# Attention with a threshold and four experts on one core: fewer and larger q/k transfers, R by heads, fillers in other banks, a held pace, highs on GpSimd

## The chip, the cores and the metric

The kernel runs on one core of a Trainium2 chip. The time is the device time in microseconds of one execution. A run of several executions gives a median; the profile is of one execution, recorded apart.

## The reference

```python
scores = scale * q @ k.T                        # 4 batches, 8 heads, 576 x 64, scale = 1/8
thresh = max(scores, axis=-1) - tau
scores = where(scores >= thresh, scores, -1e9)
attn = softmax(scores)                          # + 1e-9 under the fraction
x = (attn @ v).transpose(0, 2, 1, 3).reshape(2304, 512)
p = domain_probs / (domain_probs.sum(-1) + 1e-9)
for e in range(4):                              # w1[e]: 512 x 1024, w2[e]: 1024 x 512
    out += p[:, e] * (relu(x @ w1[e]) @ w2[e])
```

All inputs and the output are fp32.

## The kernel before

The matmuls of experts 0 and 1 are made from halves: a number is scaled by a power of two (from a sum of squares, so that fp16 can hold it), its **high** is the fp16 rounding, its **low** the rest, and a product is high x high + high x low + low x high. The power is found by `squares` (one instruction with an accumulator for each block), `total` (a matmul with ones that adds over partitions) and `pow2` (five small DVE steps).

Attention runs in 80 **items**, each 128 rows of q of a pair of heads (or the 64 tail rows of it): scores into the one score tile `S` (PE, lines 1004 to 1016), scaling and row minimum into `SS` (DVE, line 1066), the threshold by GpSimd (line 1079), the exponent by ScalarE (line 1087), the mask and the row sum by DVE (line 1096). Batch 0 goes in fp32 with turns on PE into the `b` banks (`t_prep`) and the `ma` banks. In later batches q and k are loaded (`t_load`), squared (`t_bound`), split into R16 (`t_turn`: highs on ScalarE, lows on DVE, line 771) and turned by a transposing DMA into T; the probabilities are split and turned the same way (`spread`, lines 1216, 1222 and 1179) into `PT`, and `av` (lines 1335 to 1349) takes them and v.

As soon as a 128- or 256-row part of x is whole, `unit` runs experts 0 and 1 over it (lines 1454 and 1496). When attention has ended, `w_pair` prepares the weights of experts 2 and 3 in pairs of blocks; their sums of squares go through PE into the bank `QA`. From then on `unit7` runs experts 2 and 3 by seven products in place of eight (lines 1690 and 1770).

The order of the work on each engine is made by `Plan` before anything is emitted. Every operation is recorded with an engine, an assumed duration, what it reads and writes, the buffers it uses and a priority. `Plan.schedule` then plays them through: whichever operation is ready, has its buffers and has the lowest priority number is placed next. Numbers such as `LATE` (added to a transposing DMA), `SLACK` (added to a wait between engines after the time `SLACK0`) and `pl.hold` (item i doesn't start before 6.0 us x i) only shift what stands where in the order; no wait is written into the program by them. The same holds for the assumed durations and for `port`, by which the planner lets DVE and GpSimd hold each other up. When PE has nothing ready and was busy less than `KEEP` of the recent past, the planner puts in a **filler**: four 112-column matmuls of the identity (line 1843) into columns 848 to 959 of the score tile.

Expert weights come in blocks of 128 hidden units, 128 x 1024 numbers. `w_prep` (experts 0 and 1) takes the squares, the power, the highs (line 911, ScalarE) and the lows (line 936, DVE). `on_gp` names blocks whose lows GpSimd makes instead, in two instructions: scale in place (line 919) and subtract (line 928). For expert 1 these are the four even blocks, by `GP1`.

SP's queue issues nearly all transfers, in one order: loads, stores and the transposing DMAs of R and of the probabilities.

Of the kernel before, what the change touches and what calls it, by code (L numbers as in the profile page):

```python
# [22 lines left out]
class Plan:  # L23
# [18 lines left out]
    SLACK, SLACK0, LATE, seed = {}, 0, 0, 0  # L42
# [87 lines left out]
    def schedule(self):  # L130
# [44 lines left out]
        while True:  # L175
            progress = True
            while progress:
                progress = False
                for e in engines:
# [13 lines left out]
                    if pick is None:  # L193
                        if e == "PE" and self.fill and self.fill[0] <= now < self.fill[1] and (
# [107 lines left out]
def topk_attention_moe_kernel(  # L302
# [61 lines left out]
    kind("raw", "raw", "raw", [128, 8, 2, D], FP32)  # L364
# [73 lines left out]
    def chain_tile(key, prio):
        nonlocal n_am
        if prio >= 5:  # L440
            return ("AM", key)
# [6 lines left out]
    for name in ("TP", "ET0"):  # L448
# [90 lines left out]
    def pow2(src, s_out, p_out, r, w, use, prio, tmp, au, add=None):  # L539
# [3 lines left out]
        def step(fn, rr, ww, more=()):  # L543
            dve(150, fn, rr, ww, use=use + list(more), prio=prio)
# [103 lines left out]
    def t_load(g, prio, kd="raw"):  # L648
        b, pr = divmod(g, NP)
        u = [(kd, ("qk", g))]  # L650
        for i, src in enumerate((q, k)):
# [10 lines left out]
            for h in range(2):  # L662
                load(
                    lambda i=i, h=h: pl.t(*u[0])[:, 4 * i:4 * i + 4, h, :],
                    lambda src=src, h=h: src[b, 2 * pr + h, 0:SM, :].rearrange(
                        "(p j) d -> p j d", j=4
                    ),
                    131072, [("rawqk", g, i, h)], use=u, prio=prio, issue=650, rate=175.0,
                )

    def t_bound(g, prio):
# [147 lines left out]
    def v_prep(b, loaded, prio):  # L819
        st, V = ("st", ("v", b)), ("vr", b)  # L820
        vu, view, parts = loaded
        for i in range(NP):
# [223 lines left out]
    def item(i):  # L1046
# [957 lines left out]
```

## Time and profile before

| | |
|---|---|
| median of 3 runs | 982.22 us (981.32 to 983.5) |
| profiled execution | 983.57 us, span 981.7 us |
| PE busy | 953.0 us (97% of the span) |
| DVE busy | 733.6 us (75%) |
| ACT busy | 556.5 us (57%) |
| GpSimd (POOL) busy | 257.5 us (26%) |
| fillers on PE | 228 matmuls |

The span runs from the first to the last instruction on the core. Matmuls follow each other in a pipeline, and the end of each is modelled, so a busy PE can still lose time between two of them. The granted clock is the share of TensorE's full clock that was given in a stretch. A row's "idle before" is time in which that engine stood still just ahead of the instructions of the row, and what ended it.

### The profile page before, as it was taken

What the parts mean: (1) busy time and instruction counts of PE and PEld (TensorE: products, weight loads), DVE (VectorE), ACT (ScalarE), POOL (GpSimd) and SP (SyncE); (2) the same over time, 40 slices, a digit from 0 to 9 for tenths busy, and PEclk for the clock granted to TensorE, in tenths of its full rate; (3) what the DMA queues carried; (4) which work ended last, traced back from release to release, by engine and by line L of the source; (5) the groups of instructions that cost most, each with busy time, mean ns of one, the idle gap of its engine ahead of it and who ended that gap; (6) DMA issues with size and microseconds to landing.
All of it is one profiled execution on the core that took longest, in us unless ns stands there. A gap on an engine that the chain in (4) does not pass through costs nothing.

```text
span 981.7 us, 20793 instructions
## 1 busy us (share of the span) xinstructions
PE 953.0 (97%) x7796; PEld 625.1 (64%) x7796; DVE 733.6 (75%) x1826; ACT 556.5 (57%) x1181; POOL 257.5 (26%) x400
## 2 busy tenths in 40 slices
PE   8799999999998999999999999999999999999998
PEld 6576655566655656566566756776666667666663
DVE  4799979999888988999763725897665588655551
ACT  5897877777777778786656758532222233212120
POOL 1155643354343344343332422200000010000000
PEclk9999999999999999999999999999999999999999
DMA  7812437778899679966662223301100102001001
GB/s 232 253 56 55 93 79 181 142 123 149 162 179 171 97 149 160 201 119 141 99 112 94 93 82 106 108 12 45 54 33 23 65 23 76 12 1 55 33 1 43
DMA packets 237397, 96.04 MB, mean 98 GB/s; under 512 B 201712, under 2 KB 224240, under 8 KB 237296
## 3 DMA queue, kind: packets, MB, share of 16 engines
q1 hardware_dynamic: 236208, 94.05, 43.1%
q8 instruction: 61, 1.00, 0.4%
q10 hardware_dynamic: 1088, 0.66, 0.2%
q14 instruction: 40, 0.33, 0.1%
HBM read 40.41 MB, written 14.16 MB: 56 GB/s over the span
## 4 chain that ended last, share of the span: by engine, by line
PE 77%; DVE 8%; DMA 7%; ACT 4%; issue 2%; SPq 1%; POOL 0%; DVEq 0%; ACTq 0%; POOLq 0%
PE mm L1770 19%; PE Q L1690 17%; PE mm L1496 16%; PE mm L1454 13%; PE S L1004 5%; PE av L1335 4%; DMA wraw<-in_moe_w_dram 3%; DVE E L1096 1%; DMA T<-R 1%; PE av L1344 1%; PE S L1010 1%; DVE SS L1066 1%; SPq L504 1%; DMA PT<-E 1%; ACT E L1087 1%
## 5 line engine op out<-in xcount | busy, mean ns | idle before, releaser
L1770 PE MATMUL mm<-WP,h 128*128 128x512 f16 x864 | 221.7, 379 | 0.0
L1496 PE MATMUL mm<-W,h 128*128 128x512 f16 x864 | 208.0, 381 | 0.1
L1454 PEld LDWEIGHTS <-W 128*128 128x128 f16 x2016 | 174.5, 98 | 31.4 <-issue 1.8
L1690 PEld LDWEIGHTS <-WP 128*128 128x128 f16 x1680 | 153.5, 98 | 63.5 <-issue 0.2
L1731 ACT ACTIVATE h<-qt 128x256 f16<-128x256 f32 (+1 forms) x160 | 62.1, 394 | 216.0 <-DVE qt L1710 215.6
L1454 PE MATMUL mm<-X,W 128*128 128x256 f16 (+1 forms) x1632 | 181.3, 267 | 0.0
L1710 DVE SCALAR_TENSOR_TENSOR qt<-Q,wc,qt 128x256 f32<-128x256 f32 (+1 forms) x280 | 124.2, 453 | 60.8 <-PE Q L1690 57.9
L1481 POOL TENSOR_TENSOR h<-hr,h 128x256 f16<-128x256 f32 (+1 forms) x168 | 130.1, 780 | 134.0 <-ACT h L1474 105.1
L1096 DVE SCALAR_TENSOR_TENSOR E<-SS,sm,E 128x576 f32<-128x576 f32 x144 | 123.7, 869 | 12.8 <-ACT E L1087 6.6
L1496 PEld LDWEIGHTS <-h 128*128 128x128 f16 x864 | 81.8, 99 | 77.9 <-issue 3.4
L1079 POOL TENSOR_SCALAR sm<-sm,tau_p 128x1 f32<-128x1 f32 x144 | 76.5, 532 | 184.1 <-DVE SS L1066 119.4
L1087 ACT ACTIVATE E<-SS,sm 128x576 f32<-128x576 f32 x144 | 109.1, 769 | 26.0 <-DVE SS L1066 17.6
L1770 PEld LDWEIGHTS <-h 128*128 128x128 f16 x864 | 82.9, 98 | 54.9
L1690 PE MATMUL Q<-T,WP 128*128 128x256 f16 (+1 forms) x960 | 117.8, 262 | 0.0
L1216 ACT ACTIVATE E<-E,ri 128x576 f16<-128x576 f32 (+1 forms) x120 | 83.1, 723 | 28.7 <-DVE ri L1194 11.4
L1222 DVE SCALAR_TENSOR_TENSOR E<-E,ri,E 128x576 f16<-128x576 f32 (+1 forms) x120 | 89.8, 779 | 8.6 <-ACT E L1216 8.0
L1066 DVE TENSOR_SCALAR_CACHE_REDUCE SS<-S,qc 128x576 f32<-128x576 f32 x108 | 85.7, 808 | 8.6 <-PE S L1010 3.4
L1466 ACT ACTIVATE hr<-mm,wc 128x256 f32<-128x256 f32 (+1 forms) x168 | 72.6, 435 | 33.4 <-PE mm L1454 30.5
L1690 PE MATMUL Q<-X,WP 128*128 128x256 f16 (+1 forms) x720 | 88.9, 262 | 0.0
L1647 POOL TENSOR_SCALAR psc<-pnv,wpm 128x2 f32<-128x2 f32 (+1 forms) x20 | 10.1, 505 | 287.2 <-DVE acc L1788 260.4
L1738 DVE SCALAR_TENSOR_TENSOR h<-qt,h 128x256 f16<-128x256 f32 (+1 forms) x160 | 61.4, 393 | 28.1 <-ACT h L1731 26.1
L1004 PE MATMUL S<-T 64*128 64x512 f16 (+3 forms) x440 | 71.8, 427 | 4.3 <-DVE SS L1066 4.0
(146 smaller groups left out, 1021.6 us busy)
## 6 DMA issues: line engine op xcount, KB each, us to landing
wraw<-in_moe_w_dram SPq DMA_DIRECT2D x64, 256.0 KB, 4.3
part<-acc SPq DMA_DIRECT2D x18, 256.0 KB, 2.6
X<-x_dram SPq DMA_DIRECT2D x9, 512.0 KB, 3.7
acc<-part SPq DMA_DIRECT2D x18, 256.0 KB, 3.9
out_dram<-acc SPq DMA_DIRECT2D x16, 256.0 KB, 2.3
x_dram<-X SPq DMA_DIRECT2D x7, 512.0 KB, 3.1
vr<-in_v_dram SPq DMA_DIRECT2D x12, 256.0 KB, 5.4
raw<-in_q_dram SPq DMA_DIRECT2D x24, 128.0 KB, 3.1
```

The lines of the kernel that those rows point to most:

```text
L1004: nc.tensor.matmul(ps[:, 1024 * h:1024 * h + SM] if j < 4 else ps[rows(h), 0:SM], qm(h, a), km(h, c), start=(y == 0), stop=(y == last),)
L1066: nc.vector.tensor_scalar(out=pl.t(*ssu)[:, S * h:S * h + S], in0=pl.t(*su)[:, 960 * h:960 * h + S], scalar1=qc[:, g, 2:3] if g >= NP * T3 ...
L1087: lambda h=h: nc.scalar.activation(out=pl.t(*eu)[:, S * h:S * h + S], in_=pl.t(*ssu)[:, S * h:S * h + S], func=ACTF.Exp, scale=-1.0, bias= ...
L1096: lambda h=h, col=col: nc.vector.scalar_tensor_tensor(out=pl.t(*eu)[:, S * h:S * h + S], in0=pl.t(*ssu)[:, S * h:S * h + S], scalar=pl.t(* ...
L1216: nc.scalar.activation(out=o, in_=e, func=ACTF.Copy, scale=pl.t(*ru)[:, h:h + 1])
L1222: nc.vector.scalar_tensor_tensor(out=o, in0=e, scalar=pl.t(*ru)[:, h:h + 1], in1=hh, op0=ALU.mult, op1=ALU.subtract,)
L1454: nc.tensor.matmul(ps[:, 0:n], w[:, wp, 0, c * 128:(c + 1) * 128], x[:, c, xp, c0:c0 + n], start=(i == 0), stop=(i == len(seq) - 1),)
L1481: lambda hu=hu, hru=hru: nc.gpsimd.tensor_tensor(out=pl.t(*hu)[:, 1, 0:n], in0=pl.t(*hru)[:, 0:n], in1=pl.t(*hu)[:, 0, 0:n], op=ALU.subtra ...
L1496: nc.tensor.matmul(ps, h[:, hp, 128 * i:128 * i + 128], w[:, wp, 1, :], start=(f == f0 and hp == 0 and wp == 0), stop=(f == f1 - 1 and hp ...
L1690: nc.tensor.matmul(reg(r), w[:, wp, o:o + 128], xb(b, c, xp), start=(n == 0), stop=(n == 5),)
L1710: lambda: nc.vector.scalar_tensor_tensor(out=tmp(o), in0=reg(r), scalar=wcs, in1=tmp(i), op0=ALU.mult, op1=ALU.add),
L1770: nc.tensor.matmul(ps, ht()[:, hp, 128 * i:128 * i + 128], w[:, wp, o:o + 512], start=(f == 0 and hp == 0 and wp == 0), stop=(f == NF - 1 ...
```

## The change

- `t_load`: q and k of a pair of heads in batches 1 to 3 each come in one transfer of 256 KB (pieces of 1 KB) instead of two of 128 KB (pieces of 256 bytes). The raw tile now has the two heads apart.
- `t_turn`: highs and lows of R head by head, 512 columns each, instead of 1024 at once. `t_bound` squares the same numbers.
- Fillers, and the sums of the early `total`s, go into a `b` bank that is free at the time (`ID`, `AMB`) instead of the score tile. Fillers end for good when the first expert matmul is placed.
- `w_prep`: the highs of expert 0's eight blocks are made by GpSimd; `GP1` names no block any more, so DVE makes all 16 lows.
- `v_prep`: all 16 squares of v on ScalarE instead of DVE.
- The planner's numbers: hold 6.7 us x i - 40 us, `LATE` 1500 (was 1200), `LATL` 1500 for loads (new), `SLACK` 100 for DVE and ACT from 10 us on, a seed that varies each assumed duration by about 3%, other assumed durations for a few DVE steps, `port` for the small scales of `unit`.

`P32 = 12` names the same 12 groups, those of batch 0, that `V32` named.

```diff
@@ schedule
-                        if e == "PE" and self.fill and self.fill[0] <= now < self.fill[1] and (
+                        if e == "PE" and self.fill and filling and spare["b"] and self.fill[0] <= now < self.fill[1] and (
...
+                        filling = filling and self.kinds[u[0]][0] != "mm"
...
+                        elif now >= self.SLACK0:
+                            end += self.LATL
...
-    pl.LATE = 1200
-    pl.SLACK0 = 60000
-    pl.seed = 0
+    pl.LATE, pl.LATL = 1500, 1500
+    pl.SLACK0 = 10000
+    pl.seed = 5
...
-    kind("raw", "raw", "raw", [128, 8, 2, D], FP32)
+    kind("raw", "raw", "raw", [128, 2, 8, D], FP32)
@@ t_load
-            for h in range(2):
-                load(
-                    lambda i=i, h=h: pl.t(*u[0])[:, 4 * i:4 * i + 4, h, :],
-                    lambda src=src, h=h: src[b, 2 * pr + h, 0:SM, :].rearrange(
-                        "(p j) d -> p j d", j=4
-                    ),
-                    131072, [("rawqk", g, i, h)], use=u, prio=prio, issue=650, rate=175.0,
-                )
+            load(
+                lambda i=i: pl.t(*u[0])[:, :, 4 * i:4 * i + 4].rearrange("p h j d -> p h (j d)"),
+                lambda src=src: src[b, 2 * pr:2 * pr + 2, 0:SM, :].rearrange(
+                    "h (p j) d -> p h (j d)", j=4
+                ),
+                262144, [("rawqk", g, i)], use=u, prio=prio,
+            )
@@ t_turn
-        for c, n, u in ((0, 1024, ru), (8, 256, tl)):
+        for c, n, u in ((0, 512, ru), (4, 512, ru), (8, 256, tl)):
@@ v_prep
-                lambda: junk[:, 0:9 * D], parts, [("vm", b, i)], [vu[i], st], prio, i in (0, 1, 2, 3),
+                lambda: junk[:, 0:9 * D], parts, [("vm", b, i)], [vu[i], st], prio, i in (),
@@ w_prep
-            act(
+            if (e, f) in tuple((0,f) for f in range(8)):
+                gp(
+                    1116,
+                    lambda u=u, W=W, f=f: nc.gpsimd.tensor_scalar(
+                        out=pl.t(*W)[:, 0], in0=pl.t(*u), scalar1=wsc[:, e, f:f + 1],
+                        scalar2=1.0, op0=ALU.mult, op1=ALU.mult,
+                    ),
+                    rr, [("wh", e, f)], use=[u, W], prio=prio(f),
+                )
+            else:
+              act(
@@ item
-        pl.hold[o] = (0,6.0)[0] + 1000 * (0,6.0)[1] * i
+        pl.hold[o] = (-40000,6.7)[0] + 1000 * (-40000,6.7)[1] * i
@@ the main part
-        def idle():
+        def idle(t):
             for _ in range(4):
-                nc.tensor.matmul(s_all[:, 848:960], ident16, ident16[:, 0:112], start=True, stop=True)
+                nc.tensor.matmul(t[:, 0:112], ident16, ident16[:, 0:112], start=True, stop=True)
...
-        GP1 = lambda f: f % 2 == 0
+        GP1 = lambda f: f in ()
```

Three places in the order. On GpSimd (POOL) in the early stage, before: thresholds `sm`, the differences `h` of the first unit, and between them the pair of expert 1's first blocks (lines 919 and 928).

```order
L1079 TENSOR_SCALAR sm<-sm,tau_p 128x1
L1481 TENSOR_TENSOR h<-hr,h 128x128
L919 TENSOR_SCALAR wraw_789<-wraw_789,wsc 128x1024
L1481 TENSOR_TENSOR h<-hr,h 128x128
L928 TENSOR_TENSOR W<-wraw_789,W 128x1024
L1481 TENSOR_TENSOR h<-hr,h 128x128
```

And of the changed kernel, on the same engine, a little earlier (`W<-wraw` are the highs of expert 0's blocks):

```order
L1095 TENSOR_SCALAR sm<-sm,tau_p 128x1 x6
L917 TENSOR_SCALAR W<-wraw_369,wsc 128x1024
L917 TENSOR_SCALAR W<-wraw_382,wsc 128x1024
L917 TENSOR_SCALAR W<-wraw_400,wsc 128x1024
L917 TENSOR_SCALAR W<-wraw_416,wsc 128x1024
L1095 TENSOR_SCALAR sm<-sm,tau_p 128x1 x2
L917 TENSOR_SCALAR W<-wraw_426,wsc 128x1024
L917 TENSOR_SCALAR W<-wraw_459,wsc 128x1024
```

Four highs stand in a row ahead of two thresholds, two more behind them; the pairs of expert 1 are gone.

On DVE, the first lows of expert 0, before (`x` is the scaled `av`, `X` its low):

```order
L936 SCALAR_TENSOR_TENSOR W<-wraw_359,wsc,W 128x1024
L1390 TENSOR_TENSOR X<-x_634,X 128x128
L936 SCALAR_TENSOR_TENSOR W<-wraw_363,wsc,W 128x1024
L936 SCALAR_TENSOR_TENSOR W<-wraw_385,wsc,W 128x1024
L936 SCALAR_TENSOR_TENSOR W<-wraw_403,wsc,W 128x1024
```

And now:

```order
L951 SCALAR_TENSOR_TENSOR W<-wraw_369,wsc,W 128x1024
L1406 TENSOR_TENSOR X<-x_696,X 128x128
L951 SCALAR_TENSOR_TENSOR W<-wraw_382,wsc,W 128x1024
L951 SCALAR_TENSOR_TENSOR W<-wraw_400,wsc,W 128x1024
L1382 SCALAR_TENSOR_TENSOR x_785<-av,v_c,rb 128x128
L951 SCALAR_TENSOR_TENSOR W<-wraw_416,wsc,W 128x1024
```

The lows stand as before, nearly back to back; each reads a high that now comes from GpSimd.

On SP's queue, loads of batch 1's q and k among the first transposes of R, before:

```order
L504 DMA raw<-in_q_dram 128x4x64 x2
L504 DMA raw<-in_k_dram 128x4x64 x2
L780 DMA_TRANSPOSE T_1806<-R_1787 128x10x128
L504 DMA raw<-in_q_dram 128x4x64
L780 DMA_TRANSPOSE T_1806<-R_1787 128x10x128
L504 DMA raw<-in_q_dram 128x4x64
L504 DMA raw<-in_k_dram 128x4x64 x2
```

And now:

```order
L505 DMA raw<-in_q_dram 128x2x256
L505 DMA raw<-in_k_dram 128x2x256
L783 DMA_TRANSPOSE T_1917<-R_1864 128x10x128
L505 DMA raw<-in_q_dram 128x2x256
L783 DMA_TRANSPOSE T_1917<-R_1864 128x10x128
L505 DMA raw<-in_k_dram 128x2x256
```

The transposes stand where they stood, with half as many loads between them.

## Rows read from the trace of the kernel before

**Rows 1.** Windows: stretch, length, busy (instructions) per engine, granted clock, DMA share, GB/s.
```profile
50.00:110.00 60.00, 56.91 (x616) 40.36 (x614) 58.15 (x154) 51.13 (x112) 37.36 (x47) 1.00 0.21 55
110.00:520.00 410.00, 401.00 (x3434) 251.49 (x3433) 355.12 (x919) 306.85 (x641) 168.79 (x262) 1.00 0.75 141
520.00:625.00 105.00, 101.99 (x791) 69.39 (x790) 58.08 (x121) 74.18 (x154) 33.79 (x48) 0.98 0.27 89
625.00:975.00 350.00, 350.00 (x2526) 232.77 (x2524) 229.76 (x533) 90.81 (x214) 9.49 (x18) 1.00 0.12 38
```

**Rows 2.** Windows of the fillers alone (line 1843): PE, PEld, granted clock, DMA.
```profile
60.00:80.00 20.00, 0.00 (x0) 0.00 (x0) 1.00 0.17 54
80.00:100.00 20.00, 2.88 (x52) 2.81 (x52) 1.00 0.26 67
```

**Rows 3.** Waits of PE: for whom, us in total, times, longest.
```profile
PE av L1335 <- DMA PT<-E: 4.1, 4, 1.7
PE S L1004 <- DVE SS L1066: 4.0, 4, 1.6
...
PE QA L533 <- ACT WP L523: 2.2, 1, 2.2
```

**Rows 4.** Windows around the granted clock.
```profile
80.00:90.00 10.00, 7.87 (x82) 5.44 (x79) 8.93 (x13) 6.44 (x13) 7.79 (x5) 1.00 0.40 106
300.00:315.00 15.00, 11.47 (x95) 7.44 (x94) 10.93 (x26) 10.15 (x26) 6.45 (x9) 0.89 0.85 158
565.00:575.00 10.00, 7.75 (x39) 3.98 (x37) 4.42 (x15) 4.80 (x10) 2.42 (x4) 0.83 0.23 75
```

**Rows 5.** Groups by line, batch 0's score reads: count, busy, mean, idle before.
```profile
L1066 DVE TENSOR_SCALAR_CACHE_REDUCE SS<-S,qs 128x576 f32<-128x576 f32 x36 | 28.7, 808 | 5.0 <-PE S L1010 3.3 <-PE S L1843 1.6
```

**Rows 6.** Line 514, squares on DVE: ns min/median/max, first and last start, forms.
```profile
L514 DVE SCALAR_TENSOR_TENSOR junk<-vr x12: 745/750/1158, 94.7 to 331.6; 128x576 f16<-128x576 f32 x12
L514 DVE DVE_READ_ACCUMULATOR junk<-vr x12: 75/80/85, 95.4 to 332.2; 128x1 f32 x12
```

**Rows 7.** Timeline of DVE beside GpSimd's pairs: start, us, instruction.
```profile
70.38 3.15 DVE L936 SCALAR_TENSOR_TENSOR W<-wraw,wsc,W 128x1024 f16<-128x1024 f32 x1
...
80.79 1.98 DVE L562 TENSOR_SCALAR wsc<-st 128x2 int32<-128x2 int32 x1
...
86.80 2.38 DVE L936 SCALAR_TENSOR_TENSOR W<-wraw,wsc,W 128x1024 f16<-128x1024 f32 x1 [0.28 <-ACT W L911]
...
105.13 2.68 DVE L1096 SCALAR_TENSOR_TENSOR E<-SS,sm,E 128x576 f32<-128x576 f32 x1
```

**Rows 8.** Timeline of DVE, the same instructions earlier, undisturbed.
```profile
35.24 0.17 DVE L562 TENSOR_SCALAR wsc<-st 128x4 int32<-128x4 int32 x1
35.39 0.81 DVE L1096 SCALAR_TENSOR_TENSOR E<-SS,sm,E 128x576 f32<-128x576 f32 x1
...
37.87 1.27 DVE L936 SCALAR_TENSOR_TENSOR W<-wraw,wsc,W 128x1024 f16<-128x1024 f32 x1
```

**Rows 9.** Line 919, GpSimd's scale of a block: ns min/median/max.
```profile
L919 POOL TENSOR_SCALAR wraw<-wraw,wsc x4: 1116/1288/1772, 68.5 to 100.8; 128x1024 f32<-128x1024 f32 x4
```

**Rows 10.** DMA issues: count, KB each, median us from issue to landing.
```profile
raw<-in_q_dram SPq DMA_DIRECT2D x24, 128.0 KB, 3.1
...
raw<-in_q_dram SPq DMA_DIRECT2D x4, 256.0 KB, 3.8
```

**Rows 11.** Line 771, lows of R: ns min/median/max.
```profile
L771 DVE SCALAR_TENSOR_TENSOR R<-raw,qc,R x12: 1279/1283/1286, 112.7 to 402.4; 128x1024 f16<-128x1024 f32 x12
L771 DVE SCALAR_TENSOR_TENSOR R<-tl,qc,R x12: 473/484/893, 113.9 to 403.6; 128x256 f16<-128x256 f32 x12
```

**Rows 12.** Timeline of PE behind the last `av`.
```profile
524.87 10.52 PE L1496 MATMUL mm<-W,h 128*128 128x512 f16 x48
535.23 4.09 PE L1454 MATMUL mm<-X,W 128*128 128x256 f16 x36
...
569.88 0.38 PE L533 MATMUL QA<-st,ones 128*128 128x2 f32 x2 [2.25 <-ACT WP L523]
```

More of the change, by code (lines that the diff above doesn't have):

```diff
@@ L41 @@
     FREED, LANES, EARLY = 55, 8, 8000
-    SLACK, SLACK0, LATE, seed = {}, 0, 0, 0
+    SLACK, SLACK0, LATE, LATL, seed = {}, 0, 0, 0, 0
     START, DONE, HELD, FIRST = 600, 800, {714: 1450}, 2200
@@ L328, in topk_attention_moe_kernel @@
     pl = Plan()
-    pl.SLACK = {"PE": 700, "DVE": 0, "ACT": 0,
+    pl.SLACK = {"PE": 700, "DVE": 100, "ACT": 100,
                 "s": 0, "b": 0, "ma": 0, "mm": 0, "q": 0}
-    pl.LATE = 1200
-    pl.SLACK0 = 60000
-    pl.seed = 0
+    pl.LATE, pl.LATL = 1500, 1500
+    pl.SLACK0 = 10000
+    pl.seed = 5
     first = ctx.enter_context(ExitStack())
@@ L447, in topk_attention_moe_kernel @@
     pools["b"] = early
-    for name in ("TP", "ET0"):
+    for name in ("TP", "ET0", "ID", "AMB"):
         kind(name, "b", "b", [128, 512], FP32)
@@ L543, in step @@
         def step(fn, rr, ww, more=()):
-            dve(150, fn, rr, ww, use=use + list(more), prio=prio)
+            o = dve(205, fn, rr, ww, use=use + list(more), prio=prio)
+            if more and more[0][0] == "AMB":
+                b_users.append(o)
         if add:
@@ L674, in t_bound @@
         keys = (
-            [("rawqk", g, i, h) for i in range(2) for h in range(2)]
+            [("rawqk", g, i) for i in range(2)]
             + [("tl", b, i, 0) for i in range(3)] + [("tz", b)]
@@ L751, in t_turn @@
         keys = (
-            [("rawqk", g, i, h) for i in range(2) for h in range(2)]
+            [("rawqk", g, i) for i in range(2)]
             + [("tl", b, i, 0) for i in range(3)] + [("tz", b)]
@@ L850, in v_prep @@
         gp(600, go, ["pn", ("vp", b)], [("pnv", b)], prio=prio)
-        for pr in range(NP) if b >= V32 else ():
+        if b < V32 and P32 == 12:
+            return
+        prio += 8 if b < V32 else 0
+        for pr in range(NP):
             u = ("V", (b, pr))
@@ L1052, in item @@
             ("T16" if g >= NP * T32 else "T", g), ("S", i), ("SS", i), ("E", i), ("sm", i),
-            ("rt", gi) if g // NP < V32 else ("ri", i),
-            ("PT32" if g // NP < V32 else "PT", gi),
+            ("rt", gi) if gi < P32 else ("ri", i),
+            ("PT32" if gi < P32 else "PT", gi),
         )
-        one = g // NP < V32
+        one = gi < P32
         heads = range(2) if j < 4 else range(1)
@@ L1261, in group @@
         ru, bu, au, xu, pu, V = (
-            ("rt", gi), ("rb", gi), ("av", gi), ("x32", gi), ("PT32" if b < V32 else "PT", gi),
-            ("V32" if b < V32 else "V", (b, pr)),
+            ("rt", gi), ("rb", gi), ("av", gi), ("x32", gi), ("PT32" if gi < P32 else "PT", gi),
+            ("V32" if gi < P32 else "V", (b, pr)),
         )
         r16 = ("r16", gi)
-        one = b < V32
+        one = gi < P32
         def rec():
@@ L1328, in av_ @@
             vv, av, t = pl.t(*V), pl.t(*au), pl.t(*pu)
-            pairs = ((0, 0),) if b < V32 else ((0, 0), (0, 1), (1, 0))
+            pairs = ((0, 0),) if one else ((0, 0), (0, 1), (1, 0))
             ts = lambda r, tp, c, c0, c1: t[r, c, tp, c0:c1] if one else t[r, tp, c, c0:c1]
-            va = (lambda r, vp, x: vv[r, x, :]) if b < V32 else (lambda r, vp, x: vv[r, vp, x, :])
+            va = (lambda r, vp, x: vv[r, x, :]) if one else (lambda r, vp, x: vv[r, vp, x, :])
             for c in range(4):
@@ L1342, in av_ @@
                     r = slice(64 * h, 64 * h + 64)
-                    k = n if b < V32 or not h else nm
+                    k = n if one or not h else nm
                     nc.tensor.matmul(
```

58 lines of the change are left out of this document (29 added, 29 removed).

## The prediction

> **What bounds the kernel now.** I read the busy times by stage first, then what TensorE (PE) waited for, then the rows of the places that the diff touches. By stage [rows 1], PE is busy 56.9 of 60 us from 50 to 110, 401.0 of 410 from 110 to 520, 102.0 of 105 from 520 to 625 and 350.0 of 350 from 625 to 975. From 625 on there is nothing to win but order. Before that, the reader is to see two regimes. From 50 to 110 VectorE (DVE) is busy 58.15 of 60, so DVE sets the pace, and part of PE's busy time is fillers: 2.88 us of them from 80 to 100 alone [rows 2]. From 110 on PE is the bound, DVE has 355.1 of 410 and ScalarE (ACT) 306.9 of 410 [rows 1], and what PE loses it loses in single waits: 4.1 us for transposed probabilities (`av`), 4.0 us for the score bank that DVE has not read (`S`), 2.2 us for a sum of squares of expert 2's weights (`QA`) [rows 3]. After the longest ones the granted clock is down: 0.89 over 300 to 315, 0.83 over 565 to 575 [rows 4], which is (1 - 0.89) x 15 = 1.7 us and (1 - 0.83) x 10 = 1.7 us of matmul time.
>
> **The early stage (up to 110 us), where DVE counts.** Five edits meet there.
> 1. Fillers and chain sums leave the score tile for the `b` banks. DVE waited 1.6 us for fillers before it could read scores [rows 5]. That wait goes: -1.6. The fillers fall from 228 to 172 by the order, and none stands behind the first expert matmul, where 92 did.
> 2. The squares of v go to ACT: eight of batches 0 and 1 fall in this stage, each 0.75 us and 0.08 us for its accumulator [rows 6]: 8 x 0.83 = -6.6 on DVE.
> 3. GpSimd's pair for four blocks of expert 1 (scale, then subtract) goes. Beside it DVE instructions took far longer than alone: 3.15 and 2.38 against 1.27 for a low of W, 1.98 against 0.17 for a step of a power, 2.68 against 0.81 for an exponent's mask [rows 7, 8]. Together 1.9 + 1.1 + 1.8 + 1.9 = 6.7 us that come back: -6.7.
> 4. The four lows go to DVE instead: 4 x 1.27 [rows 8] = +5.1.
> 5. The eight highs of expert 0 move from ACT to GpSimd. The trace has no such instruction; nearest is GpSimd's scale of the same 128x1024 block, 1.12 to 1.77 us [rows 9]. In the order four of them stand in a row, and DVE's four lows, which stood back to back, each follow a high, so from the second high on each pair is likely to take turns instead of overlapping: 6 x 1.12 = +6.7. Lower bound 0 (a low starts between two highs, GpSimd waits), upper bound 8 x 1.77 = +14.2. I take 6.7: [rows 7] show four such waits of 1.1 to 1.9 us each, so a whole short one is the nearest. ACT gives up eight highs of 1024 columns and takes eight squares of 576; it has 8.9 us free in the 60 [rows 1], so I cost that at nothing.
>
> The Trainium skill ("SBUF — State Buffer", section "Who interferes with whom") speaks against edit 5: a DVE instruction with two SBUF inputs and a GpSimd instruction that reads SBUF block each other whole, whoever is second. [Rows 7, 8] agree: a low of 1.27 us became 3.15 beside GpSimd's subtraction. By the rule alone all eight highs would wait in turn with the lows, which is the upper end above rather than my 6.7.
>
> Sum on DVE: -1.6 - 6.6 - 6.7 + 5.1 + 6.7 = -3.1. Before 50 us the stage is bound by loads as well, so I pass on half: **-1.5**. Bounds: -9.8 (no lock) to +4.4 (the full lock).
>
> **The middle (110 to 520).** q and k come in one transfer per pair: 24 issues instead of 48 on SP's queue, pieces of 1 KB instead of 256 bytes. 128 KB in small pieces took 3.1 us to land, 256 KB in large ones 3.8 [rows 10], so a pair's q is whole after 3.8 us rather than after two transfers in a row. What waits behind these issues on SP are the transposes of R and of the probabilities, and they are what `av` and, through T, `S` wait for. The two waits are 8.1 us [rows 3], and the dip at 300 another 1.7. The trace doesn't say how much of this the loads cause: between 0 and -9.8. The planner now also counts loads and transposes later (`LATE` and `LATL` 1500, `SLACK` 100), which places the consumer further behind. I take half: **-4.9**. The Trainium skill ("DMA: Bandwidth & Descriptors", "Specifications") puts the smallest piece at line rate at 512 bytes; by it the old loads paid extra for every piece, and the sum would go toward -9.8. The two landing times do point that way.
>
> Head-by-head R costs DVE a fixed part more per pair. From 1283 ns for 1024 columns and 484 for 256 [rows 11] it is 0.22 us; 12 pairs make +2.6. Against it stand the squares of v of batches 2 and 3, 8 x 0.83 = -6.6. Both lie beside PE work on a DVE that is 87% busy: 0. If that cover were gone the net would be -4.0.
>
> **The pace and the turn to experts 2 and 3.** Item i of attention is held to 6.7 i - 40 us instead of 6.0 i: later from item 57 on. In the order 240 + 192 matmuls of experts 0 and 1 (256 and 512 columns) stand behind the last `av`, where 336 + 240 stood. At 4.09/36 and 10.52/48 us each [rows 12] that is 96 x 0.114 + 48 x 0.219 = 21 us less cover for the weights of experts 2 and 3. PE has other work either way, so this costs nothing by itself, unless a weight is late. Against that, the sums `QA` now stand further apart: 48 + 36 matmuls between the first two before (14.6 us), 45 + 84 now (45 x 0.219 + 84 x 0.114 = 19.4). The wait of 2.2 us at 569.9 [rows 3, 12] and its dip of 1.7 should shrink; but the fifth and sixth sums move close behind the fourth. Bounds -3.9 to +3.9; I take **-2.0**. The last 7 us are untouched.
>
> **Sum.** -1.5 - 4.9 - 2.0 = -8.4 us. The profiled execution took 983.57 us (span 981.7), so 975.2 in its terms; the median of the runs shown is 982.22, so the forecast is 982.22 - 8.4 = 973.8, say **974**.
>
> **Rivals.**
> A. All waits go. The lock of edit 5 stays away and every wait of [rows 3] and both dips go: -9.8 - 9.8 - 3.9 = -23.5, 959; with two thirds of it, 966. For it: PE has no other reason to stand still. Against: nearly all rows of the order have moved, and a new order brings new waits.
> B. Nothing. PE was busy 98% from 110 to 520 [rows 1], and the DVE time that is saved lies beside it; the waits move to other places: 982. For it: a wait of 1.7 us here and there is what any order of such density leaves. Against: SP's queue really loses 24 issues.
> C. Slower, by the clock. Fillers end with the first expert matmul. In 80 to 100 us 52 of them stood [rows 2], and even with them PE was busy 7.87 of 10 in 80 to 90 [rows 4]; the stretch 300 to 315, where the granted clock fell, had 11.47 of 15. If the clock drops to 1.2 GHz from about 60 us and stays until PE is full, every us there does half the matmuls. About 6 us of loss are absorbed by what were fillers and idle time (2.9 + 3.1, from [rows 1, 2]). So it decides against the forecast from 2 x (6 + 8.4) = 29 us at the low level. Over 50 us it is 25 - 6 = +19, and the time 982.2 - 8.4 + 19 = 993. A single dip of 10 to 15 us stays inside the forecast. For it: no fillers from 60 on. Against: from 60 to 80 there are no fillers before either, and the clock is 1.00 [rows 2].
>
> **How the numbers follow.** Forecast 0.52 (966 to 980.2), A 0.16, B 0.14, C and whatever else is slower 0.18. A measurement of this kernel can tell about 0.2% (2 us) from no change. B falls inside 980.3 to 984.2 mostly, with a little to each side: faster 0.69, same 0.12, slower 0.19. The range leaves about one in ten at each end: 962 to 987. The forecast's own range is 966 to 980.
>
> **What would show it.** Right: no wait of DVE for fillers; no step of a power or mask of 0.2 and 0.81 us drawn out to 2 us between 60 and 110; PE's waits for `av` and `S` together under 5 us; the granted clock 1.00 at 300 and at 570. Edit 5 is mis-sized if lows of W run at 1.27 us beside the highs (too dear) or over 2.4 us (too cheap). Wrong as a whole: a granted clock under 0.9 between 60 and 130 us (C), a wait of PE for a square of WP longer than 3 us behind the last `av` (the turn), or PE waits in 110 to 520 of the same 8 us in other places (B).

## The result, and the profile after

The changed kernel took 968.42 us (median of 4 runs, 967.93 to 969.01) against 981.77 us for the kernel before: a ratio of 0.987 (95% interval 0.985 to 0.989). The forecast was 974, its own range 966 to 980.2. The profiled execution took 968.05 us, its span is 966.2.

By stage (stretch, length, then busy time and instructions of PE, PEld, DVE, ACT and POOL, granted clock, DMA share, GB/s; answers to [rows 1]):

```profile
50.00:110.00 60.00, 54.92 (x530) 37.82 (x527) 54.84 (x151) 46.80 (x113) 31.77 (x43) 0.97 0.19 54
110.00:520.00 410.00, 404.93 (x3467) 255.76 (x3465) 351.86 (x905) 315.92 (x671) 169.75 (x266) 1.00 0.70 141
520.00:580.00 60.00, 60.00 (x498) 42.81 (x497) 26.18 (x54) 39.13 (x86) 18.45 (x28) 1.00 0.31 93
...
609.00:960.00 351.00, 350.12 (x2532) 233.47 (x2530) 236.15 (x552) 95.51 (x221) 6.00 (x18) 1.00 0.11 38
```

PE gained 3.9 us of busy time from 110 to 520 and stands still nowhere from 520 to 580. DVE no longer is full from 50 to 110 (54.84 in place of 58.15).

What PE waited for from 110 to 520 us (us, times, longest; answers to [rows 3]):

```profile
PE S L1020 <- DVE SS L1082: 3.0, 6, 1.0
...
PE av L1351 <- DMA PT<-E: 0.2, 1, 0.2
```

The 8.1 us of `av` and `S` in [rows 3], all of them between 110 and 520 us, became 3.2, and the wait for `QA` is gone. The longest wait that is left is early: over the whole span `S` has 6.5 us in 8 waits, 3.3 of it in one near 60 us.

The clock at the places of [rows 4], and where it is down now:

```profile
60.00:70.00 10.00, 8.60 (x80) 6.64 (x81) 9.10 (x30) 7.61 (x22) 6.80 (x10) 0.83 0.18 58
...
300.00:315.00 15.00, 13.73 (x100) 6.61 (x100) 12.19 (x39) 14.81 (x37) 3.20 (x8) 1.00 0.80 130
565.00:575.00 10.00, 10.00 (x130) 8.46 (x129) 2.38 (x8) 9.28 (x25) 3.88 (x8) 1.00 0.22 70
```

The dips at 300 and 570 are gone, and one has come between 60 and 70, behind the long wait for `S`; it is worth (1 - 0.83) x 10 = 1.7 us of matmul time. What led to it, from the timeline (start, us, instruction, in brackets the idle time before and what ended it):

```profile
53.97 2.21 POOL L917 TENSOR_SCALAR W<-wraw,wsc 128x1024 f16<-128x1024 f32 x2
55.12 3.33 DVE L951 SCALAR_TENSOR_TENSOR W<-wraw,wsc,W 128x1024 f16<-128x1024 f32 x2 [1.02 <-POOL W L917]
...
59.20 0.81 DVE L1082 TENSOR_SCALAR_CACHE_REDUCE SS<-S,qs 128x576 f32<-128x576 f32 x1
...
60.52 0.81 DVE L1082 TENSOR_SCALAR_CACHE_REDUCE SS<-S,qs 128x576 f32<-128x576 f32 x1
...
61.40 1.33 PE L1020 MATMUL S<-T 64*128 64x512 f32 x4 [3.28 <-DVE SS L1082]
```

GpSimd makes the last highs of expert 0, DVE waits 1.02 us for one, takes 3.33 us for two lows, and only then, after some small steps, reads the scores (two heads); PE waits 3.28 us for the bank.

**Lost time by stage.** To see where the gain came from I count every matmul of the work at the distance from start to start that its shape usually has at full clock (0.109 us for 128x256 in fp16, 0.216 for 128x512, and so on, the same numbers for all kernels). Fillers don't count. That gives some 900 us of work, the same in every kernel here; the total hangs on the distances chosen, the differences between the rows hardly do. The time up to a point less the work started by then is **lost**: waits, fillers and low clock together. It is worked out from one profiled execution each, which was 1.8 us above the median for the kernel before and 3.0 below it for seed1, so differences of a microsecond or two say little.

| lost us | to 110 | 110-280 | 280-310 | 310-520 | 520-580 | to 900 in all |
|---|---|---|---|---|---|---|
| before | 37.5 | 13.1 | 6.5 | 12.4 | 3.9 | 74.7 |
| after | 34.4 | 11.2 | 3.2 | 9.4 | 0.1 | 59.2 |
| *after's order, one edit undone* | | | | | | |
| highs_act | 33.2 | 12.2 | 2.3 | 11.4 | 0.4 | 60.1 |
| two_1k | 33.7 | 11.3 | 5.5 | 10.3 | 0.2 | 61.8 |
| loads_two | 34.1 | 13.3 | 5.2 | 11.0 | 0.2 | 64.6 |
| vsq_dve | 36.2 | 12.6 | 5.0 | 9.5 | 0.2 | 64.4 |
| pairs_gp | 39.6 | 11.6 | 2.7 | 10.8 | 0.3 | 65.7 |
| v_act | 34.0 | 15.1 | 3.7 | 11.5 | 0.2 | 65.2 |
| *planned anew* | | | | | | |
| hold_old | 35.7 | 12.2 | 2.3 | 11.6 | -0.3 | 61.8 |
| seed1 | 38.1 | 11.6 | 7.7 | 8.6 | 0.2 | 65.9 |
| seed1_v_act | 37.0 | 11.0 | 8.8 | 10.8 | 0.2 | 67.8 |
| seed0 | 37.8 | 14.1 | 5.5 | 12.6 | 0.2 | 70.0 |
| numbers_old | 34.8 | 12.1 | 7.9 | 10.0 | 4.3 | 70.2 |
| before_numbers | 35.3 | 13.0 | 12.0 | 10.5 | 0.3 | 72.0 |

So the 15.5 us between the two traces are 3.1 up to 110, 8.2 from 110 to 520 (3.3 of it in the 30 us at 280) and 3.8 in the turn; by the medians the gain is 13.4.

### The profile page after: what moved, and what is told of

Same layout as the page of the kernel before. It is cut to its first block, busy times and chain, and to the rows that moved or that the text cites. A ratio compares the mean times of both kernels' runs of the same rounds, so it can differ in the third digit from the quotient of the medians.

```text
span 966.2 us, 20685 instructions
## 1 busy us (share of the span) xinstructions
PE 945.1 (98%) x7740; PEld 622.7 (64%) x7740; DVE 724.0 (75%) x1810; ACT 558.6 (58%) x1217; POOL 253.9 (26%) x400
## 4 chain that ended last, share of the span: by engine, by line
PE 76%; DVE 9%; ACT 5%; DMA 4%; issue 3%; SPq 2%; POOL 1%; DVEq 0%; ACTq 0%; POOLq 0%
PE mm L1786 19%; PE Q L1706 17%; PE mm L1470 14%; PE mm L1512 13%; PE S L1020 4%; PE av L1351 4%; DVE E L1112 2%; SPq L505 2%; DVE SS L1082 1%; ACT junk L524 1%; PE S L1026 1%; PE ET L1133 1%; DVE E L1238 1%; PE av L1360 1%; ACT E L1103 1%
## 5 line engine op out<-in xcount | busy, mean ns | idle before, releaser
L1786 PE MATMUL mm<-WP,h 128*128 128x512 f16 x864 | 219.4, 379 | 0.0
L1512 PE MATMUL mm<-W,h 128*128 128x512 f16 x864 | 204.5, 379 | 1.6 <-ACT hr L1482 1.6
L1497 POOL TENSOR_TENSOR h<-hr,h 128x256 f16<-128x256 f32 (+1 forms) x168 | 134.2, 805 | 140.7 <-ACT h L1490 96.2
L1112 DVE SCALAR_TENSOR_TENSOR E<-SS,sm,E 128x576 f32<-128x576 f32 x144 | 121.2, 852 | 14.1 <-ACT E L1103 6.8
L1103 ACT ACTIVATE E<-SS,sm 128x576 f32<-128x576 f32 x144 | 109.2, 771 | 25.6 <-DVE SS L1082 17.9
L1095 POOL TENSOR_SCALAR sm<-sm,tau_p 128x1 f32<-128x1 f32 x144 | 70.1, 488 | 176.9 <-DVE SS L1082 116.4
L1238 DVE SCALAR_TENSOR_TENSOR E<-E,ri,E 128x576 f16<-128x576 f32 (+1 forms) x120 | 92.4, 800 | 10.2 <-ACT E L1232 9.8
L1232 ACT ACTIVATE E<-E,ri 128x576 f16<-128x576 f32 (+1 forms) x120 | 82.8, 722 | 17.5 <-DVE ri L1210 11.6
L1663 POOL TENSOR_SCALAR psc<-pnv,wpm 128x2 f32<-128x2 f32 (+1 forms) x20 | 6.6, 332 | 290.7 <-DVE acc L1804 254.0
```

The lines of the kernel that those rows point to most:

```text
L1103: lambda h=h: nc.scalar.activation(out=pl.t(*eu)[:, S * h:S * h + S], in_=pl.t(*ssu)[:, S * h:S * h + S], func=ACTF.Exp, scale=-1.0, bias= ...
L1112: lambda h=h, col=col: nc.vector.scalar_tensor_tensor(out=pl.t(*eu)[:, S * h:S * h + S], in0=pl.t(*ssu)[:, S * h:S * h + S], scalar=pl.t(* ...
L1232: nc.scalar.activation(out=o, in_=e, func=ACTF.Copy, scale=pl.t(*ru)[:, h:h + 1])
L1238: nc.vector.scalar_tensor_tensor(out=o, in0=e, scalar=pl.t(*ru)[:, h:h + 1], in1=hh, op0=ALU.mult, op1=ALU.subtract,)
L1497: lambda hu=hu, hru=hru: nc.gpsimd.tensor_tensor(out=pl.t(*hu)[:, 1, 0:n], in0=pl.t(*hru)[:, 0:n], in1=pl.t(*hu)[:, 0, 0:n], op=ALU.subtra ...
L1512: nc.tensor.matmul(ps, h[:, hp, 128 * i:128 * i + 128], w[:, wp, 1, :], start=(f == f0 and hp == 0 and wp == 0), stop=(f == f1 - 1 and hp ...
```

## The experiments

Two theories went in. One: the edits take waits away, and what they take stays away in any order. The other: the order that the planner's numbers and the seed make decides, and the edits only matter within it. Seven experiments keep an order, six that of the changed kernel and one that of seed 1, and change only what is issued at a place (PE's matmuls come in the very same order in all six as in after); the others let the planner plan anew. Each run had the kernel before run beside it, with medians from 979.3 to 981.4 us, so a difference in us between two runs is good to about 2 us; the ratios to before are the safer measure.

**1 and 2. The cross of edits and numbers.**

```diff
 numbers_old: the changed kernel with
-    pl.SLACK = {"PE": 700, "DVE": 100, "ACT": 100, ...
-    pl.LATE, pl.LATL = 1500, 1500
-    pl.SLACK0 = 10000
-    pl.seed = 5
+    pl.SLACK = {"PE": 700, "DVE": 0, "ACT": 0, ...
+    pl.LATE = 1200
+    pl.SLACK0 = 60000
+    pl.seed = 0
-        pl.hold[o] = (-40000,6.7)[0] + 1000 * (-40000,6.7)[1] * i
+        pl.hold[o] = (0,6.0)[0] + 1000 * (0,6.0)[1] * i
 before_numbers: the kernel before with the reverse, and the line that adds LATL
```

> The changed kernel with the planner's numbers of before (hold 6.0 us x i, LATE 1200, no LATL, SLACK 0, no seed); every edit of the instructions stays, the order is planned anew. If the gain comes from the edits themselves (fewer transfers, squares on ScalarE, fillers in other banks), most of it stays: 969 to 973 us. If it comes from the order that the numbers make (consumers placed further behind, the held pace), most of it goes: 977 to 983 us, with PE's waits for av and S from 110 to 520 us back at about 8 us and a wait behind the last av.

Measured: 979.42 us, ratio to before 0.999 (0.9971 to 1.0008).

> The other half of the cross: the kernel before with the planner's numbers of the changed one (hold 6.7 us x i - 40 us, LATE and LATL 1500, SLACK 100 from 10 us on, seed 5), no instruction edited. If the edits bring the gain: 979 to 983 us. If the order does: 970 to 975 us. If the two need each other, both halves of the cross stay near 978.

Measured: 979.15 us, 0.9995 (0.9976 to 1.0013). Neither half does anything that can be measured; only both together, with seed 5, do. That speaks against the first theory, and for "need each other" or for luck with one order. Two things fall out by stage. The loss in the turn hangs on the numbers alone (3.9 and 4.3 with the old, 0.1 to 0.3 with the new), here with the old ones, the window and PE's wait:

```profile
520.00:580.00 60.00, 56.57 (x415) 37.15 (x415) 28.91 (x66) 36.06 (x72) 14.55 (x20) 1.00 0.27 84
```

```profile
PE QA L534 <- ACT WP L524: 2.1, 2, 1.5
```

And from 280 to 310 both lose more than before (7.9 and 12.0 against 6.5). In before_numbers:

```profile
285.00:300.00 15.00, 11.88 (x93) 7.05 (x93) 12.65 (x32) 10.64 (x23) 3.58 (x11) 0.77 1.08 183
```

**3. The highs of expert 0 back on ScalarE** (order kept).

```diff
-                    lambda u=u, W=W, f=f: nc.gpsimd.tensor_scalar(
-                        out=pl.t(*W)[:, 0], in0=pl.t(*u), scalar1=wsc[:, e, f:f + 1],
-                        scalar2=1.0, op0=ALU.mult, op1=ALU.mult,
+                    lambda u=u, W=W, f=f: nc.scalar.activation(
+                        out=pl.t(*W)[:, 0], in_=pl.t(*u), func=ACTF.Copy, scale=wsc[:, e, f:f + 1]
```

> The changed kernel in its own order, with one thing undone: the eight highs of expert 0 are issued by ScalarE at the same places in place of GpSimd. If the lock and the queue on GpSimd cost what the trace shows (two lows of 2.13 in place of 1.27 us, 1.0 us of waiting for a high, 3.3 us of PE waiting for the score bank near 60 us and a clock of 0.83 behind it), this is faster by 2 to 4 us: 964 to 966.5, with no low over 1.3 us. Rival: ScalarE has no room for 8 x 1.14 = 9.1 us more and its copies and exponents come late: 968 to 972.

Measured: 969.01 us, 0.9883 (0.9856 to 0.991): no difference that can be told, so the expected 2 to 4 us missed. The mechanism was there: lows (line 950 here, ns min/median/max), then the clock from 60 to 70:

```profile
L950 DVE SCALAR_TENSOR_TENSOR W<-wraw,wsc,W x16: 1272/1282/1485, 37.1 to 105.9; 128x1024 f16<-128x1024 f32 x16
```

```profile
60.00:70.00 10.00, 9.22 (x118) 7.28 (x117) 9.90 (x31) 8.50 (x23) 7.46 (x11) 1.00 0.17 56
```

The longest low takes 1.49 us instead of 2.13, the dip is gone and 1.2 us less is lost up to 110. In their place PE waited for ScalarE's copies up to 110 (3.4 us at `rp`, where after has 0.4):

```profile
PE rp L1314 <- ACT PT L1041: 3.4, 4, 2.1
```

And 3.0 us more were lost from 110 to 280 and from 310 to 520 (1.0 and 2.0). Edit 5 moved the wait from one engine to another.

**4 and 5. The loads of q and k in two transfers** (order kept; 48 issues; loads_two with the old layout and 256-byte pieces, two_1k with pieces of 1 KB).

```diff
-            load(
-                lambda i=i: pl.t(*u[0])[:, :, 4 * i:4 * i + 4].rearrange("p h j d -> p h (j d)"),
...
+            def two(i=i, src=src):
+                for h in range(2):
+                    nc.sync.dma_start(
+                        out=pl.t(*u[0])[:, 4 * i:4 * i + 4, h, :],
+                        in_=src[b, 2 * pr + h, 0:SM, :].rearrange("(p j) d -> p j d", j=4),
+                    )
```

> The changed kernel in its own order, with the old loads of q and k: two transfers of 128 KB per tensor and pair with 256-byte pieces at the place of each single one, 48 issues in place of 24. If the loads held up the transposes behind them on SP's queue: 3 to 8 us slower (971 to 976), with PE waits for transposed probabilities and for T between 110 and 400 us. If the order has room enough: within 1 us of 968.4.

Measured: 974.26 us, 0.9936 (0.9913 to 0.996), 5.8 us slower than after.

> The changed kernel in its own order, with two transfers of 128 KB in place of each single one (48 issues), but in pieces of 1 KB: it tells the issues from the pieces. With both undone the time was 974.3. If the issues on SP's queue hold up the transposes behind them: 972 to 975. If the 256-byte pieces do (18,816 more packets): 968 to 970.

Measured: 970.82 us, 0.9892 (0.9864 to 0.9921): between, and not told apart from after. By the medians 2.4 of the 5.8 us go with the issues and 3.4 with the pieces, but the intervals leave that open. In loads_two PE never waits for a transpose itself, though that was expected; it waits for the score bank, 5.6 us from 110 to 520, against 3.0 in after. Of the 5.4 us more that are lost in all, 2.0 lie between 280 and 310, where the transposes are late; windows, then DVE and PE in time:

```profile
285.00:300.00 15.00, 12.75 (x115) 9.88 (x113) 10.62 (x31) 10.22 (x24) 6.67 (x9) 0.89 1.02 260
```

```profile
291.07 0.82 DVE L1082 TENSOR_SCALAR_CACHE_REDUCE SS<-S,qc 128x576 f32<-128x576 f32 x1 [3.49 <-DMA PT<-E]
```

```profile
292.96 0.82 PE L1020 MATMUL S<-T 64*128 64x512 f16 x6 [2.25 <-DVE SS L1082]
```

The three buffers of `SS` are shared with the halves of R and of the probabilities (`E16`) that the transposes read. A transpose that lands late keeps a buffer, DVE can't read the scores, PE can't write new ones, and the clock is 0.89 over the 15 us.

**6. The held pace alone undone** (planned anew).

```diff
-        pl.hold[o] = (-40000,6.7)[0] + 1000 * (-40000,6.7)[1] * i
+        pl.hold[o] = (0,6.0)[0] + 1000 * (0,6.0)[1] * i
```

> The changed kernel with item i held to 6.0 us x i as before, all other numbers as now (planned anew). If the held pace is what removes the wait for the weights of expert 2 behind the last av (4 us of 520 to 580 us, which both kernels with the new numbers have won and the one with the old numbers has not): that loss is back, 972 us or more, with PE waiting for a square of WP near 570. If it is the other numbers: no such wait, 967 to 970.

Measured: 968.61 us, 0.9877 (0.9847 to 0.9906), the same as after, with no wait of PE between 520 and 640 us. The pace is not what mended the turn; of the numbers `LATE`, `LATL` and `SLACK` are left (both other seeds keep the turn whole too), and I did not part them. The order is also not a wholly new one: 6232 of PE's 7568 matmuls (fillers left out) stand at the same place as in after, against 5067 with seed 0 and 4378 with seed 1.

**7 and 8. Another seed** (planned anew, `pl.seed = 0` and `1` in place of 5).

> The changed kernel with seed 0 (assumed durations not varied) in place of 5, nothing else. It sizes what the order alone is worth. If the edits and numbers bring the gain, any seed keeps it: 966 to 971. If the seed is a part of it (a lucky order round 285 to 315 us), 972 to 980, with the loss in that stretch.

Measured: 978.94 us, 0.9979 (0.9959 to 0.9999). numbers_old had seed 0 as well (0.999), so with that seed the other numbers are worth nothing that can be told.

> The changed kernel with seed 1, as a second draw of the same order. As for seed 0: 966 to 971 if the gain does not hang on the seed, 972 to 980 if it does; the two draws and seed 5 together give the spread.

Measured: 978.27 us, 0.9969 (0.995 to 0.9988). With every edit and every number of the changed kernel but the seed, some 10 of the 13.4 us are gone. The seed only varies assumed durations by about 3%. The clock is a part of the difference, but not the most of it: executions with the same mean granted clock of 0.998 took 968.05 and 969.01 us in after, 975.6 and 978.89 in seed1. In seed1, DVE's and PE's longest wait and the clock behind them:

```profile
301.95 0.82 DVE L1082 TENSOR_SCALAR_CACHE_REDUCE SS<-S,qc 128x576 f32<-128x576 f32 x1 [4.06 <-DMA PT<-E]
```

```profile
304.31 0.82 PE L1020 MATMUL S<-T 64*128 64x512 f16 x6 [3.85 <-DVE SS L1082]
```

```profile
300.00:315.00 15.00, 11.15 (x89) 6.66 (x87) 11.34 (x30) 12.06 (x28) 7.12 (x10) 0.89 0.43 84
```

It is the same chain as in loads_two, with after's loads.

**9 and 10. Loads of v of batches 2 and 3 on ScalarE's queue** (order kept, of seed 1 and of after). In after SP issues the six loads of batch 3 in a row, ahead of transposes; in seed 1 they stand between 290 and 299 us, with transposes among them and not in a row.

```profile
290.37 5.18 SPq L505 DMA_DIRECT2D vr<-in_v_dram  x6
295.65 16.85 SPq L1195 DMA_TRANSPOSE PT<-E  x8
```

```diff
+        def vload(out_, in_, nbytes, w, **kw):
+            eng = nc.scalar if b > 1 else nc.sync
+            pl.op("SP", 475, lambda: eng.dma_start(out=out_(), in_=in_()), (), w, xfer=nbytes / 320.0, **kw)
```

> The order of seed 1 (978.3 us), with one thing moved: the six loads of v of batch 2 and the six of batch 3 are issued by ScalarE's queue at the same places instead of by SP's. In every order so far SP issues the six loads of batch 3 near 290 us in a row (4 to 5 us), with stores of x ahead of them and transposes of probabilities behind; DVE, then PE, wait for these transposes (5.1 and 4.5 us), and seed 1 loses 7.7 us from 280 to 310. If SP's queue is the cause: that loss falls to about 3, and the time to 973 to 975. Rival: the DMA engines themselves are full there (a share of 1.06 to 1.10 from 285 to 300 us in every kernel), so the transposes are as late as before: 977 to 980.

Measured: 976.98 us, 0.9963 (0.9947 to 0.9979), and 8.8 us lost from 280 to 310 (7.7 in seed1).

> The same move of v's loads to ScalarE's queue in the changed kernel's own order (seed 5). If SP's queue counts: what is left of the loss from 280 to 310 (3.2 us) shrinks, 965.5 to 967.5, the best version so far. If the DMA engines are the bound, or this order has room enough on SP: 968 to 970, a little slower where ScalarE's own work waits behind an issue.

Measured: 972.66 us, 0.9922 (0.9899 to 0.9946), slower than after. The theory of SP's queue fell: with six issues fewer there the loss did not shrink. The stretch from 285 to 300, in seed1_v_act and in v_act:

```profile
285.00:300.00 15.00, 10.24 (x78) 7.07 (x76) 10.06 (x27) 6.37 (x11) 4.30 (x7) 0.78 0.98 234
```

```profile
285.00:300.00 15.00, 13.31 (x130) 9.94 (x128) 11.09 (x29) 10.96 (x25) 5.30 (x9) 1.00 1.18 261
```

A DMA share of about 1 fits the rival, that the engines themselves are full, but nothing here took bytes away to test it. The times to landing speak for it. Of v_act's loss 3.9 us lie between 110 and 280, where the loads of batch 2 moved too. There the transposes issued at 161.9 and 163.6 us now have four loads of v in flight beside them, from ScalarE's queue; in after those loads stand behind such transposes, at 166.4 to 169.2. Issues, transfers and median us from issue to landing, in v_act from 161 to 165 and in after from 162 to 166:

```profile
PT<-E SPq DMA_TRANSPOSE x2, 7.9
```

```profile
PT<-E SPq DMA_TRANSPOSE x2, 3.6
```

PE waits 2.0 and 2.1 us for these transposes (none there in after). So the one order of SP's queue seems to have also kept loads out of the way of transposes.

**11. GpSimd's pair for expert 1's even blocks again** (order kept).

```diff
+                if e == 1 and f % 2 == 0:
+                    nc.gpsimd.tensor_scalar(out=pl.t(*u), in0=pl.t(*u), scalar1=wsc[:, e, f:f + 1], ...)
+                    nc.gpsimd.tensor_tensor(out=pl.t(*W)[:, 1], in0=pl.t(*u), in1=pl.t(*W)[:, 0], op=ALU.subtract)
+                    return
...
```

> The changed kernel in its own order, with the lows of expert 1's even blocks made by GpSimd's pair again (scale, then subtract) in place of DVE. The prediction has this edit at -6.7 + 5.1 = -1.6 us of DVE time up to 110 us, half of it passed on. By that: 969 to 970, and masks, lows or power steps of DVE drawn out to 2 or 3 us beside the pair. Rival: the pair's other cost counts more, GpSimd is busy 1.1 + 2.1 us for each block and the thresholds behind it come late, 971 to 974. Or DVE has the four lows to spare: 967 to 968.5.

Measured: 975.44 us, 0.9954 (0.9936 to 0.9972), 7.0 us slower than after, 5.2 of them lost up to 110: the rival. One chain shows it, from the timeline, and the window behind it:

```profile
93.98 2.13 POOL L955 TENSOR_TENSOR W<-wraw,W 128x1024 f16<-128x1024 f32 x1
94.15 3.05 DVE L959 SCALAR_TENSOR_TENSOR W<-wraw,wsc,W 128x1024 f16<-128x1024 f32 x1 [1.20 <-ACT W L926]
...
96.10 2.29 POOL L1106 TENSOR_SCALAR sm<-sm,tau_p 128x1 f32<-128x1 f32 x1
...
98.35 1.80 POOL L1508 TENSOR_TENSOR h<-hr,h 128x128 f16<-128x128 f32 x2
...
99.80 0.37 ACT L1493 ACTIVATE hr<-mm,wc 128x128 f32<-128x128 f32 x1 [3.80 <-POOL h L1508]
...
100.47 0.26 ACT L1053 COPY PT<-ET 128x128 f32<-128x128 f32 x1
...
100.77 4.54 PE L1362 MATMUL av<-PT,V 128*64 128x320 f32 x16 [2.85 <-ACT PT L1053]
```

```profile
100.00:110.00 10.00, 9.23 (x50) 4.72 (x51) 5.66 (x23) 7.96 (x25) 2.64 (x6) 0.66 0.00 0
```

The differences `h` stand behind the pair and a threshold that takes 2.29 us (0.27 when undisturbed), ScalarE waits 3.80 us for one, its copy of `PT` behind that is late, PE waits 2.85 us, and the clock is 0.66 from 100 to 110. That one chain is 2.85 us of wait and (1 - 0.66) x 10 = 3.4 us of matmul time. Beside the pair three of DVE's lows took 2.8, 2.8 and 3.05 us.

**12. The squares of v back on DVE** (order kept).

```diff
+            if w[0][0] == "vm":
+                nc.vector.scalar_tensor_tensor(
+                    out=junk(), in0=src(), scalar=1.0, in1=src(), op0=ALU.mult, op1=ALU.mult,
+                    accum_out=dst(),
+                )
...
```

> The changed kernel in its own order, with all 16 squares of v made by DVE again, at the same places. The prediction has this edit at 8 x 0.83 = 6.6 us of DVE time up to 110 us, half of it passed on, and at nothing for the eight in the middle. By that: 970 to 973, with 2 to 4 us more lost up to 110 us and no more from 110 to 520. If DVE has that time to spare where the squares stand: 967.5 to 969. If DVE's slack in the middle is gone too (it is busy 86% there): 974 or more, with waits of PE for the score bank.

Measured: 973.51 us, 0.9926 (0.9897 to 0.9956), 5.1 slower: 1.8 us more lost up to 110 and 3.3 from 110 to 520, where the prediction had nothing. The windows, and PE's waits from 110 to 520:

```profile
60.00:70.00 10.00, 8.12 (x68) 6.48 (x69) 8.30 (x29) 5.91 (x15) 5.15 (x10) 0.66 0.25 79
...
110.00:520.00 410.00, 402.75 (x3454) 255.01 (x3453) 358.65 (x928) 310.81 (x651) 173.88 (x269) 1.00 0.70 140
```

```profile
PE S L1023 <- DVE SS L1085: 6.0, 4, 3.1
```

The 6.8 us more of DVE are as costed; PE's wait for the score bank doubles from 3.0 to 6.0 us. A part of the 5.1 is the clock: it was 0.989 to 0.996 in the six executions here and 0.996 to 0.998 in the four of after, and the two at 0.996 took 970.19 and 971.37 us.

## Why the prediction was right, and where not

The time lay inside the forecast's own range, and faster was the likeliest sign. The total is righter than its reasons.

**Early stage, -1.5 forecast, 3.1 less lost.**
- Fillers (-1.6): right on the wait, not on its worth. DVE's score reads of batch 0 now wait for nothing but scores (answers to [rows 5]); but the idle time ahead of them went from 5.0 to 6.6 us, since the wait for scores doubled from 3.3 to 6.6. This edit was not tried alone.

```profile
L1082 DVE TENSOR_SCALAR_CACHE_REDUCE SS<-S,qs 128x576 f32<-128x576 f32 x36 | 28.5, 811 | 6.6 <-PE S L1026 6.6
```

- The pair gone, lows on DVE (-6.7 and +5.1, half passed on: -0.8): mis-sized. It is worth 7.0 us in this order. I priced only DVE's drawn-out instructions (three lows by 4.8 us in pairs_gp); the dearer part was what queued behind the pair on GpSimd, and the low clock with it.
- Edit 5 (+6.7): too dear. Six of expert 0's eight lows ran at about 1.27 us, two at 2.13; with the wait for one high that is 2 x 0.86 + 1.02 = 2.7.

```profile
L951 DVE SCALAR_TENSOR_TENSOR W<-wraw,wsc,W x16: 1269/1279/2132, 37.2 to 107.0; 128x1024 f16<-128x1024 f32 x16
...
L917 POOL TENSOR_SCALAR W<-wraw,wsc x8: 1112/1135/2153, 35.0 to 55.1; 128x1024 f16<-128x1024 f32 x8
```

The full lock of the Trainium skill ("SBUF — State Buffer", "Who interferes with whom") shows where a low and a high meet: the low that starts at 39.45 us, beside a high from 39.37, takes 2.13 us in place of 1.27. By that rule alone the prediction let all eight highs wait in turn with the lows, the upper end of its range; two lows and two highs were drawn out.

- Squares of v (-6.6, half passed on: -3.3): 1.8 up to 110 when undone, with the clock at 0.66 instead of 0.83 over 60 to 70.

**Middle, -4.9 forecast, 8.2 less lost.** The old loads do cost time, 5.8 us when they come back, and transposes are late in the one stretch shown. That the 24 issues on SP are the reason, as the prediction had it, is not shown: with 48 issues of large pieces the time can't be told from after, and taking other issues off SP did not help. Head-by-head R took what was costed (24 x 0.750 - 12 x 1.283 = 2.6 us of DVE), and was not undone alone:

```profile
L774 DVE SCALAR_TENSOR_TENSOR R<-raw,qc,R x24: 739/750/1182, 114.5 to 399.4; 128x512 f16<-128x512 f32 x24
```

"Both lie beside PE work on a DVE that is 87% busy: 0" was the step that failed here: the squares of v in this stretch cost 3.3 us from 110 to 520, half of the 6.6 us that they take on DVE. A mean of 87% hides stretches with none.

**The turn, -2.0 forecast, 3.8 less lost.** The whole wait and its dip went. The held pace is not needed for it. That the sums `QA` stand further apart fits: from the first to the fourth it is 52.6 us in after and 50.0 in hold_old, where before had 45.2, 2.25 of them the wait. But it is not the whole of it: before_numbers has 46.1 and no wait, numbers_old 47.5 with a wait of 1.5. What decides is open.

**The halves.** "I take half" stood for not knowing what an order does, and all three parts treated the order as neutral. That is the step that failed as a whole. The seed alone moves the time by 10 us, more than my forecast of the whole change; other orders of the same edits stand at 978 to 979, which is near rival B (982), while the one that was built came near the milder case of A (966). B's reason ("the waits move to other places") holds for seeds 0 and 1, A's for seed 5, and neither could be read from before's trace. In after's own order, undoing the loads, the pair and the squares costs 5.8 + 7.0 + 5.1 = 17.9 us, each tried alone, more than the 13.4 of the whole change. So in this order the gain stands on these edits, and by the other two seeds they are not enough for it. That the gain can't be had without them is not shown: the kernel before was drawn again only once (before_numbers), and no edit was undone with a new order made for what is left. Why seed 5 keeps clear of the late transposes at 280 to 310 is open.

**Rival C**: the clock does fall behind the first expert matmuls, 0.83 over 60 to 70, but in one dip, which the text left inside the forecast; over 60 to 130 it is 0.98. By the letter of its sign (under 0.9 between 60 and 130) C would have come; in its sense, a low clock that stays, it did not.

**The signs.** No masks or power steps were drawn out between 60 and 110: over the whole run the longest mask took 1.29 us, where [rows 7] had 2.68.

```profile
L1112 DVE SCALAR_TENSOR_TENSOR E<-SS,sm,E x144: 798/814/1294, 12.9 to 514.6; 128x576 f32<-128x576 f32 x144
```

`av` and `S` together are 3.2 us from 110 to 520 (under 5; with the early wait of 3.3 the whole run has 6.7), the clock at 300 and 570 is 1.00, and the edit-5 sign reads "too dear".

No version measured here beats the changed kernel: highs_act and hold_old equal it, and two_1k can't be told from it.

## What to carry to other kernels

When a change makes a planner draw a new order, price the edits and the draw apart: plan the same edits with two or three other seeds, and undo each edit with the order kept. An edit that was tested in one order only says what it is worth there; here the same set was worth nothing measurable with one set of numbers, 0.2 to 0.3% with two seeds and 1.3% with a third. The one that was kept is then partly a lucky draw, and is to be called so. And an engine's mean busy share doesn't say that work on it is hidden: look at the stretches in which the next engine already waits for it.

## What the runs showed of the hardware

- A PE wait of some 2 to 4 us often goes with a stretch at the lower clock, 1.2 GHz: 3.28 us and 0.83 over 60 to 70 (after), 2.85 and 0.66 over 100 to 110 (pairs_gp), 3.85 and 0.89 over 300 to 315 (seed1). In matmul time these three are (1 - 0.83) x 10 = 1.7, 3.4 and (1 - 0.89) x 15 = 1.7 us. Not always: behind 3.06 us at 181.7 in vsq_dve the clock stayed at 1.00. While it was low in pairs_gp, the 16 `av` matmuls took 4.54 us; in after, the same 16 took 2.37:

```profile
115.66 2.37 PE L1351 MATMUL av<-PT,V 128*64 128x320 f32 x16
```

- GpSimd's one-input scale of 128x1024 and DVE's two-input low draw each other out by up to 0.9 and 1.0 us when they meet (2132 and 2153 ns against about 1270 and 1115).
- Moving loads from SP's queue to ScalarE's did not bring SP's transposes forward while the DMA share was about 1 (0.98 and 1.18). Where such loads then ran beside them, two transposes took 7.6 and 8.3 us to land, with a median of 3.3 over the run (v_act).
